# Attention scores of three batches as three half-array products per head, instead of two full-array or one single precision product

## The chip, the core and the metric

The kernel runs on one core of a Trainium2 chip. The metric is the device time of one execution in microseconds, smaller is better. The core's engines run side by side and meet only through semaphores: TensorE (PE: matrix products and transposes, whose weight loads are listed apart as PEld), VectorE (DVE), ScalarE (ACT), GpSimd (POOL), and SyncE (SP), which starts the DMA transfers.

## What is computed

An attention over 4 batches of 8 heads (576 tokens, 64 numbers per head), masked by blocks of 64 tokens, feeds two layers of gated and mixed matrix products:

```python
scores = (q @ k.T) / sqrt(64)            # per batch and head, 576 x 576
scores = where(block_i >= block_j, scores, -1e9)
attn = exp(scores - max(scores)); attn = attn / (sum(attn) + 1e-9)
x = attn @ v                             # 2304 tokens x 512
x = (sigmoid(x @ w_gate) * (x @ w_val)) @ w_out          # first layer, inner width 1536
out = sum over e of p[:, e:e+1] * (relu(x @ w1[e]) @ w2[e])   # second layer, 4 experts of 1024
```

All inputs are single precision. The factors on q and k are such that the scores must be kept to more than one reduced product's precision.

## The kernel before, in words

**Work.** The kernel has three parts. The attention makes x, batch by batch, and writes it to memory (`xd`). The first layer (`l1_1`, `l2_1`) runs in four passes, one for each batch of x; the second layer (`l1_items`, `l2_items`, `l2s_items`) follows. While pass p of the first layer runs, the attention of batch p+1 is woven in: `attn_to` hands out attention steps in proportion to the pass, and a scheduler of the framework then sets the final order on each engine. In pass 0 the weights of the first layer are also read, split into a high and a low part and written back (`raw`, `wa` to `wd`, `wo`).

**Two kinds of product.** TensorE knows a native single precision product (both operands float32), which runs as two passes and has two records in the trace, and a reduced one (float32r). Where precision is wanted from reduced products, a number is split into a high part `hi` and a low part `lo` (the rest), and hi·hi + hi·lo + lo·hi is summed in PSUM. Both layers do that with full-array products (128 rows by 128 columns, 288 to 512 columns streamed).

**Attention, by pairs of heads.** A batch has four pairs (g counts them over all batches: 0 to 15). A pair's q and k come from memory with tokens on partitions (`qn`, `kn`); TensorE transposes them in parts (`prep_tr`, two parts of q, two of k, each into a PSUM bank `tbank`), so that a pair's two heads lie on rows 0-63 and 64-127; ScalarE and VectorE copy them out. Then come the scores by query tile t: t = 0 to 3 have 128 query rows and 128, 256, 384 and 512 key columns, each head for itself, and t = 4 has the last 64 queries of both heads against all 576 keys in two halves of 288 columns. Row maximum (VectorE), exponential (ScalarE), transposes of the result (`pt` into `tbank`), and the product with v (`obank`, two half arrays by columns, native single precision) follow.

Before, the pairs have two forms:

- Form "N" (batches 0 and 1). q and k stay float32, one ScalarE copy for each part. A score tile is one native product on the 64 rows of its head; `side_by_side` puts the two heads' products next to each other, on the upper and lower half of the array. t = 4 is four native products on quarters of the array for each half (64 rows by 64 columns).
- Form "F" (batches 2 and 3). For head h one tile holds q's high part on rows 0-63 and its low part on rows 64-127; the k tile holds the high part twice; a third tile (`klz`) holds k's low part on rows 0-63 and zeros below. So two full-array reduced products give hi·hi + lo·hi and hi·lo. The heads follow one another. The copies out of `tbank` work on 64 rows each: 2 on ScalarE and 2 on VectorE for a part of q, 4 and 2 for a part of k. t = 4 takes four reduced products for each half.

Scores of batches 1 to 3 go to two PSUM banks `s`; the transposes share two banks `t`; the first layer's products use `c1`, `c2` and `lo`. Each `lo` group of six products must wait until VectorE has added the group before it into x (line 884).

**Order.** Every engine works through one queue in the order that the scheduler gave. The attention's steps stand between the first layer's groups of six products.

Of the kernel before, what the change touches and what calls it, by code (L numbers as in the profile page):

```python
# [24 lines left out]
UB = 1  # L25
LATE = (0, 1, 2)
# [36 lines left out]
def attention_moe_moe_kernel(  # L63
# [18 lines left out]
    P = 128  # L82
# [62 lines left out]
    klz = []  # L145
# [6 lines left out]
    def attn_items(segs):  # L152
# [30 lines left out]
        def load(g, nm, src, c0, c1):  # L183
            _, b, pr, seg = pairs[g]
            if nm == "v":
                t = vts[g % 2]
            elif nat_of(g):
                if nm == "k" and pr % 2:
                    t = attn.tile([P, 5 * P], F32, tag="tk", name="kn", bufs=3)
                    t = t.rearrange("p (c h d) -> p c h d", c=5, h=2)  # L190
                else:
                    tag = "kn" if nm == "k" else ("qn", "vn")[pr % 2]
                    t = attn.tile([P, 5, 2, D], F32, tag=tag, name=f"{nm}n")
            else:
                t = attn.tile([P, 5, 2, D], F32, tag=f"{nm}n", name=f"{nm}n")
# [18 lines left out]
        def prep_alloc(g):  # L214
            if nat_of(g):
                prep[g] = dict(
                    tq=attn.tile([P, S], F32, tag="tq", name="tqn", bufs=3),
                    tk=attn.tile([P, 5 * P], F32, tag="tk", name="tkn", bufs=3)[:, :S])
                return
            prep[g] = dict(  # L220
                tq=[attn.tile([P, S], F32R, tag="tq", name="tq", bufs=3) for _ in range(2)],
                tk=[attn.tile([P, 5 * P], F32R, tag="tk", name="tk", bufs=3)[:, :S] for _ in range(2)])

        def prep_tr(g, nm, cs):
# [14 lines left out]
            elif nm == "q":  # L239
                t0, t1 = d["tq"]  # L240
                nc.scalar.activation(out=t0[0:64, sl], in_=tbank[0:64, :o], func=AF.Copy, scale=SCALE)
                nc.scalar.activation(out=t1[0:64, sl], in_=tbank[64:128, :o], func=AF.Copy, scale=SCALE)
                nc.vector.scalar_tensor_tensor(
                    out=t0[64:128, sl], in0=tbank[0:64, :o], scalar=SCALE, in1=t0[0:64, sl].bitcast(F32),
                    op0=ALU.mult, op1=ALU.subtract)
                nc.vector.scalar_tensor_tensor(
                    out=t1[64:128, sl], in0=tbank[64:128, :o], scalar=SCALE, in1=t1[0:64, sl].bitcast(F32),
                    op0=ALU.mult, op1=ALU.subtract)
            else:
# [1184 lines left out]
```

## Time and profile before

| what | value |
|---|---|
| median of 3 runs | 1415.74 us (1414.04 to 1418.02) |
| the profiled execution's own time | 1417.34 us |
| its span in the profile | 1415.6 us |
| TensorE busy / VectorE / ScalarE / GpSimd | 1373.8 / 983.1 / 780.7 / 480.4 us |
| weight loads (PEld) busy | 1266.7 us |
| stretch of the scores of batches 0 and 1 | 8 to 77 us and 77 to 175 us |
| of batches 2 and 3 | 184 to 313 us and 318 to 426 us |

The table is read thus: one engine, TensorE, is busy for 97% of the span; the others have room on average. A busy TensorE is not one at its peak, because a record of a product lasts longer than the distance to the next one. In the rows below the distance between two starts on TensorE is therefore what a piece of work takes, and the middle number of a timeline row (its us) is not.

### The profile page before, as it was taken

How to read it: one execution, taken by the hardware profiler on the slowest of the kernel's cores; microseconds unless marked ns; L12 is line 12 of the kernel's file. 1: busy time of each engine (PE TensorE's matmuls, PEld its weight loads, DVE VectorE, ACT ScalarE, POOL GpSimd, SP SyncE). 2: the span in 40 equal slices, each digit the busy share in tenths (PEclk: the TensorE clock that was granted, in tenths of full speed). 3: DMA queues.
4: the chain of work that ended last, by engine and by line, in shares of the span. 5: the costliest groups of instructions: out<-in, count | busy, mean ns of one | idle time of the engine just before them, and what ended most of it. 6: DMA issues, size and time to landing. Idle time of an engine off the chain costs nothing.

```text
span 1415.6 us, 26232 instructions
## 1 busy us (share of the span) xinstructions
PE 1373.8 (97%) x9212; PEld 1266.7 (89%) x9212; DVE 983.1 (69%) x2103; ACT 780.7 (55%) x1926; POOL 480.4 (34%) x502
## 2 busy tenths in 40 slices
PE   5889999999999999999999999999999999999998
PEld 3447788889899999999999989989999999999998
DVE  6867789986766445467777666757766687766766
ACT  5878788888876433343445445445444454443442
POOL 4544345312112100012576556533322342322322
PEclk8989999999999999999999999999999999999999
DMA  7988787767756888898799888886676777676754
GB/s 227 311 243 277 218 278 264 246 204 214 217 178 229 306 296 267 282 364 311 264 336 358 296 300 302 281 308 227 226 254 249 249 266 278 246 269 231 276 205 157
DMA packets 213683, 371.93 MB, mean 263 GB/s; under 512 B 75568, under 2 KB 140080, under 8 KB 207408
## 3 DMA queue, kind: packets, MB, share of 16 engines
q1 hardware_dynamic: 212464, 369.99, 77.1%
q8 instruction: 74, 1.21, 0.3%
q14 instruction: 57, 0.47, 0.1%
q10 hardware_dynamic: 1088, 0.26, 0.1%
HBM read 269.00 MB, written 101.19 MB: 262 GB/s over the span
## 4 chain that ended last, share of the span: by engine, by line
PE 83%; DMA 5%; DVE 5%; ACT 3%; issue 2%; SPq 1%; POOL 1%; DVEq 0%; ACTq 0%; POOLq 0%
PE c L119 37%; PE o L119 25%; PE lo L119 7%; PE s L119 4%; PE obank L119 3%; PE t L119 2%; PE tbank L458 2%; DMA raw<-in_moe_w_out_dram 1%; DMA raw<-in_moe_w_gate_dram 1%; PE s L349 1%; DMA wa<-w1d 1%; ACT pt L382 1%; DMA w1g<-w1d 1%; PE tbank L229 1%; POOL wt L653 1%
## 5 line engine op out<-in xcount | busy, mean ns | idle before, releaser
L119 PE MATMUL c<-xc,w1g 128*128 128x384 f32 x1920 | 384.8, 338 | 2.1 <-DMA w1g<-w1d 1.8
L119 PEld LDWEIGHTS c<-xc,w1g 128*128 128x128 f32 x1920 | 330.4, 188 | 8.8 <-DVE hb L1062 1.3
L119 PE MATMUL o<-w2s,hb 128*128 128x256 f32 x1728 | 243.5, 282 | 1.1 <-DVE acc L1211 1.1
L119 PEld LDWEIGHTS o<-w2s,hb 128*128 128x128 f32 x1728 | 231.8, 189 | 2.0 <-DVE acc L1211 1.7
L1211 DVE SCALAR_TENSOR_TENSOR acc<-o,pr_t,acc 128x256 f32<-128x256 f32 x264 | 123.4, 479 | 57.9 <-PE o L119 55.7
L1071 POOL TENSOR_TENSOR hs<-hf 128x384 f32<-128x384 f32 x64 | 64.1, 1023 | 287.1 <-ACT hf L1079 255.7
L119 PE MATMUL lo<-g,wo 128*128 128x288 f32 x888 | 148.0, 300 | 4.8 <-DVE x L884 4.8
L119 PE MATMUL o<-w,hb 128*128 128x512 f32 x576 | 142.9, 391 | 0.0
L119 PEld LDWEIGHTS lo<-g,wo 128*128 128x128 f32 x888 | 125.8, 188 | 9.6 <-DVE x L884 6.7
L1079 ACT ACTIVATE hf<-c 128x384 f32<-128x384 f32 x128 | 65.7, 513 | 115.7 <-DVE c L1116 58.4
L119 PEld LDWEIGHTS o<-w,hb 128*128 128x128 f32 x576 | 107.2, 188 | 18.5 <-DVE acc L1155 0.3
L1116 DVE TENSOR_TENSOR c<-c,snap 128x384 f32<-128x384 f32 x144 | 77.9, 553 | 55.8 <-PE c L119 38.9
L1109 ACT ACTIVATE snap<-c 128x384 f32<-128x384 f32 x144 | 65.8, 485 | 85.6 <-PE c L119 85.4
L1060 ACT ACTIVATE hb<-hs 128x384 fp32r<-128x384 f32 x128 | 63.3, 518 | 65.0 <-POOL hs L1071 64.9
L1062 DVE TENSOR_TENSOR hb<-hs,hb 128x384 fp32r<-128x384 f32 x128 | 87.1, 695 | 5.8 <-ACT hb L1060 5.4
L884 DVE TENSOR_TENSOR x<-lo,x 128x288 f32<-128x288 f32 x124 | 55.6, 452 | 45.6 <-PE lo L119 45.0
L119 PE MATMUL c<-xc,wa 128*128 128x288 f32 x504 | 82.6, 299 | 0.9 <-DMA wa<-w1d 0.5
L382 ACT ACTIVATE pt<-s,nm 128x128 f32<-128x128 f32 (+3 forms) x128 | 67.4, 530 | 17.2 <-DVE nm L380 14.5
L119 PEld LDWEIGHTS c<-xc,wa 128*128 128x128 f32 x504 | 71.2, 188 | 3.1 <-DMA wa<-w1d 0.8
L119 PE MATMUL c<-xc,wc 128*128 128x288 f32 x432 | 71.0, 299 | 1.1 <-ACT snap L808 1.1
L458 PE MATMUL tbank<-ident,pt 128*128 128x128 f32 x320 | 55.3, 287 | 17.2 <-ACT pTa L445 9.9
L808 ACT ACTIVATE snap<-c 128x288 f32<-128x288 f32 x108 | 44.2, 409 | 43.8 <-PE c L119 43.2
(173 smaller groups left out, 2697.5 us busy)
## 6 DMA issues: line engine op xcount, KB each, us to landing
w1g<-w1d SPq DMA_DIRECT2D x96, 512.0 KB, 5.4
w2s<-w2d SPq DMA_DIRECT2D x48, 1024.0 KB, 6.5
w1d<-w1g SPq DMA_DIRECT2D x48, 512.0 KB, 5.0
wa<-w1d SPq DMA_DIRECT2D x40, 512.0 KB, 5.2
wb<-w1d SPq DMA_DIRECT2D x40, 512.0 KB, 5.3
wc<-w1d SPq DMA_DIRECT2D x40, 512.0 KB, 4.4
wo<-wod SPq DMA_DIRECT2D x36, 512.0 KB, 6.0
wr<-in_moe_w_dram SPq DMA_DIRECT2D x32, 512.0 KB, 5.4
```

Source lines behind the costliest of these rows:

```text
L119: ins = nc.tensor.matmul(out=out, lhsT=lhsT, rhs=rhs, start=start, stop=stop, skip_group_check=skip)
L382: ins = nc.scalar.activation(out=pt[:, x * nk:(x + 1) * nk], in_=sp[:, x - x0], func=AF.Exp, bias=nm[:, j0 + x:j0 + x + 1], scale=1.0, acc ...
L458: nc.tensor.transpose(out=tbank[:, x * P:(x + 1) * P], in_=pt[:, x * P:(x + 1) * P], identity=ident)
L808: nc.scalar.activation(out=t, in_=d["c1"][:, :TH1], func=AF.Copy)
L884: nc.vector.tensor_tensor(out=x2[t, dm], in0=ps, in1=x2[t, dm], op=ALU.add)
L1060: nc.scalar.activation(out=t[:, 0], in_=src, func=AF.Copy if low is None else AF.Relu)
L1062: nc.vector.tensor_tensor(out=t[:, 1], in0=src, in1=t[:, 0].bitcast(F32), op=ALU.subtract)
L1071: nc.gpsimd.tensor_tensor(out=o, in0=x, in1=y, op=op)
L1079: nc.scalar.activation(out=hf[q, blk], in_=c, func=AF.Relu)
L1109: nc.scalar.activation(out=t, in_=d["c1"][:, :TH], func=AF.Copy)
L1116: nc.vector.tensor_tensor(out=c, in0=d[tag][:, :TH], in1=d[n], op=ALU.add)
L1211: nc.vector.scalar_tensor_tensor(out=o, in0=ps, scalar=pr, in1=o, op0=ALU.mult, op1=ALU.add)
```

## The change

Batch 0 keeps form N. Batches 1, 2 and 3 get a new form "R". q and k of a pair are split into a tile `hi` and a tile `lo` of 128 rows each, with head 0 on the upper and head 1 on the lower 64 rows, by one ScalarE copy and one VectorE subtraction for each part. A score tile is three reduced products for each head on the 64 rows of that head: q-hi with k-hi, q-hi with k-lo, q-lo with k-hi. The heads alternate (head 0, head 1, head 0, ...), each into its own bank, and the first of the six waits until both banks are free. t = 4 becomes three full-array reduced products for each half. `klz` is gone, and q and k of batches 2 and 3 get a second buffer to be loaded into.

```diff
-        QTS = KTS = {"N": range(5), "F": range(5)}
+        QTS = KTS = {"N": range(5), "R": range(5)}
...
         def nat_of(g):
-            return pairs[g][3] != "F"
+            return pairs[g][3] == "N"
...
             prep[g] = dict(
-                tq=[attn.tile([P, S], F32R, tag="tq", name="tq", bufs=3) for _ in range(2)],
-                tk=[attn.tile([P, 5 * P], F32R, tag="tk", name="tk", bufs=3)[:, :S] for _ in range(2)])
+                tq=[attn.tile([P, S], F32R, tag="tq", name="tq", bufs=NB) for _ in range(2)],
+                tk=[attn.tile([P, S], F32R, tag="tk", name="tk", bufs=NB) for _ in range(2)])
...
-            elif nm == "q":
-                t0, t1 = d["tq"]
-                nc.scalar.activation(out=t0[0:64, sl], in_=tbank[0:64, :o], func=AF.Copy, scale=SCALE)
-                nc.scalar.activation(out=t1[0:64, sl], in_=tbank[64:128, :o], func=AF.Copy, scale=SCALE)
+            else:
+                hi, lo = d["tq" if nm == "q" else "tk"]
+                f = SCALE if nm == "q" else 1.0
+                nc.scalar.activation(out=hi[:, sl], in_=tbank[:, :o], func=AF.Copy, scale=f)
                 nc.vector.scalar_tensor_tensor(
-                    out=t0[64:128, sl], in0=tbank[0:64, :o], scalar=SCALE, in1=t0[0:64, sl].bitcast(F32),
-                    op0=ALU.mult, op1=ALU.subtract)
...
+                    out=lo[:, sl], in0=tbank[:, :o], scalar=f, in1=hi[:, sl].bitcast(F32), op0=ALU.mult, op1=ALU.subtract)
...
             with tc.high_priority():
-                two = mms[1][0]()
-            tc.add_manual_dep(two.ins, one.ins.name, NOSYNC, reason="heads side by side")
+                for m in range(1, len(mms) * mms[0][2]):
+                    ins = mms[m % 2][0](m // 2)
+                    tc.add_manual_dep(ins.ins, last.ins.name, NOSYNC, reason="heads side by side")
+                    last = ins
...
-                else:
-                    w = d["tq"][h]
-                    mm("s", out=sp, lhsT=w[:, qs], rhs=d["tk"][h][:, k0:k1], start=True, stop=False)
-                    mm("s", out=sp, lhsT=w[:, qs], rhs=d["kl"][h][:, k0:k1], start=False, stop=True)
+                return nc.tensor.matmul(
+                    out=sp, lhsT=d["tq"][m // 2][r, qs], rhs=d["tk"][m % 2][r, k0:k1], start=(m == 0), stop=(m == 2))
...
-                for n, k in enumerate([*d["tk"], *d["kl"]]):
-                    mm("s", out=sp, lhsT=q4[2 * (g % 2) + n % 2], rhs=k[:, k0:k1], start=(n == 0), stop=(n == 3))
+                for m in range(3):
+                    mm("s", out=sp, lhsT=q4[2 * (g % 2) + m // 2], rhs=d["tk"][m % 2][:, k0:k1], start=(m == 0), stop=(m == 2))
...
-        queue = attn_items([(0, "N"), (1, "N"), (2, "F"), (3, "F")])
+        queue = attn_items([(0, "N"), (1, "R"), (2, "R"), (3, "R")])
```

Because the scheduler sets the order anew, three places are shown as the queues now stand. The first is TensorE's queue at the first tile (t = 0, 128 columns) of batch 2's first pair; `s` are score banks, `c` and `lo` the first layer, `tbank` transposes. Before:

```order
L119 MATMUL s_2775<-tk_2540,tq_2538 128x128
L119 MATMUL s_2775<-klz0_132,tq_2538 128x128
L119 MATMUL s_2781<-tk_2541,tq_2539 128x128
L119 MATMUL s_2781<-klz1_134,tq_2539 128x128
L478 MATMUL tbank_2791<-ident_60,pt4_2550 128x128 x4
```

And in the changed kernel the same tile, where `tq_2634` and `tk_2636` are the high parts, and `tq_2635` and `tk_2637` the low ones:

```order
L120 MATMUL c1_2225<-xc7_1191,wc_2052 128x288 x6
L327 MATMUL s_2865<-tk_2636,tq_2634 128x128
L327 MATMUL s_2866<-tk_2636,tq_2634 128x128
L223 MATMUL tbank_2853<-ident_60,kn_2436 128x128 x3
L327 MATMUL s_2865<-tk_2637,tq_2634 128x128
L327 MATMUL s_2866<-tk_2637,tq_2634 128x128
L327 MATMUL s_2865<-tk_2636,tq_2635 128x128
L327 MATMUL s_2866<-tk_2636,tq_2635 128x128
L445 MATMUL tbank_2900<-ident_60,pt4_2648 128x128 x4
```

The two heads now alternate in two banks, and three full-array transposes stand between the first two products and the last four, so that the tile is two separate half-array blocks. Over the whole queue the 12 pairs of form R have 48 score tiles and 58 such blocks: 10 of the 12 tiles of 128 columns are cut in two in this way. In batch 1 there are 19 of them where 23 native blocks stood before, and in batches 2 and 3 there are 39 where none stood. The blocks of `obank` (half arrays by columns) go from 56 to 60 over the kernel.

The second place is TensorE's queue at the next tile (t = 1, 256 columns) of the same pair. Before:

```order
L119 MATMUL s_2847<-tk_2540,tq_2538 128x256
L119 MATMUL s_2847<-klz0_132,tq_2538 128x256
L119 MATMUL c1_2151<-xc4_1173,wc_1983 128x288 x6
L119 MATMUL s_2853<-tk_2541,tq_2539 128x256
L119 MATMUL s_2853<-klz1_134,tq_2539 128x256
```

And in the changed kernel:

```order
L120 MATMUL lo_2339<-g_1753,wo_1634 128x288 x3
L327 MATMUL s_2939<-tk_2636,tq_2634 128x256
L327 MATMUL s_2940<-tk_2636,tq_2634 128x256
L327 MATMUL s_2939<-tk_2637,tq_2634 128x256
L327 MATMUL s_2940<-tk_2637,tq_2634 128x256
L327 MATMUL s_2939<-tk_2636,tq_2635 128x256
L327 MATMUL s_2940<-tk_2636,tq_2635 128x256
```

The heads, which stood apart with first-layer products between them, are now one block of six.

The third place is VectorE's queue where the first part of k of the same pair is split; `x2` is the sum that releases the bank `lo`. Before:

```order
L884 TENSOR_TENSOR x2_1539<-lo_1971,x2_1539 128x288
L254 TENSOR_TENSOR klz0_132<-tbank_2699,tk_2540 64x256
L255 TENSOR_TENSOR klz1_134<-tbank_2699,tk_2541 64x256
L490 TENSOR_SCALAR nm_2396<-nm_2396 128x4
L491 RECIPROCAL nm_2396<-nm_2396 128x4
L811 TENSOR_TENSOR c_2079<-c2_2058,snap_2050 128x288
L497 COPY xr_2972<-nm_2396 128x256
L884 TENSOR_TENSOR x2_1612<-lo_2004,x2_1612 128x288
```

And in the changed kernel:

```order
L851 TENSOR_TENSOR x2_1775<-lo_2195,x2_1775 128x288
L574 SCALAR_TENSOR_TENSOR raw_2561<-raw_2561 128x512
L457 TENSOR_SCALAR nm_2488<-nm_2488 128x4
L458 RECIPROCAL nm_2488<-nm_2488 128x4
L237 SCALAR_TENSOR_TENSOR tk_2637<-tbank_2797,tk_2636 128x256
L464 COPY xr_3068<-nm_2488 128x256
L851 TENSOR_TENSOR x2_1816<-lo_2255,x2_1816 128x288
```

Between two sums into x one subtraction of 128 rows stands where two of 64 rows stood.

## Rows read from the trace of the kernel before

**Rows 1.** The page's first table: engine, busy us (share of the span), instructions.

```profile
PE 1373.8 (97%) x9212; PEld 1266.7 (89%) x9212; DVE 983.1 (69%) x2103; ACT 780.7 (55%) x1926; POOL 480.4 (34%) x502
```

**Rows 2.** Busy us by stretch: length, PE, PEld, DVE, ACT, POOL, granted clock, DMA.

```profile
97.50:107.80 10.30, 9.62 (x37) 5.29 (x38) 7.20 (x21) 7.51 (x22) 6.32 (x7) 0.50 0.63 192
107.80:180.00 72.20, 69.87 (x490) 54.42 (x488) 53.93 (x136) 59.17 (x167) 26.35 (x28) 1.00 0.80 249
180.00:310.00 130.00, 123.74 (x893) 108.65 (x893) 117.29 (x286) 109.73 (x302) 50.49 (x52) 1.00 0.77 248
310.00:430.00 120.00, 119.95 (x891) 109.21 (x891) 82.66 (x253) 97.89 (x278) 22.90 (x36) 1.00 0.66 201
225.00:265.00 40.00, 35.41 (x256) 30.92 (x255) 37.57 (x84) 32.38 (x87) 23.64 (x24) 1.00 0.78 259
```

**Rows 3.** TensorE's waits, 180 to 310 us: total us, times, longest.

```profile
PE lo L119 <- DVE x L884: 4.4, 5, 1.4
```

**Rows 4.** TensorE's timeline, batch 1, half-array block: start, us, instruction, count.

```profile
158.22 0.96 PE L119 MATMUL c<-xc,wb 128*128 128x288 f32 x6
159.12 0.70 PE L349 MATMUL s<-tkn,tqn 64*128 64x256 f32 x4
159.75 1.06 PE L119 MATMUL c<-xc,wc 128*128 128x288 f32 x6
160.65 0.38 PE L458 MATMUL tbank<-ident,pt 128*128 128x128 f32 x2
```

**Rows 5.** TensorE's timeline, a block of 128 columns in batch 1.

```profile
151.64 0.49 PE L349 MATMUL s<-tkn,tqn 64*128 64x128 f32 x4
152.06 0.66 PE L458 MATMUL tbank<-ident,pt 128*128 128x128 f32 x4
152.48 0.78 PE L119 MATMUL lo<-g,wo 128*128 128x288 f32 x4
```

**Rows 6.** TensorE's timeline, both halves of the last query rows in batch 1.

```profile
166.97 1.19 PE L349 MATMUL s<-tkn,tqn 64*64 64x288 f32 x8
168.08 1.07 PE L119 MATMUL c<-xc,wa 128*128 128x288 f32 x6
```

**Rows 7.** The timeline of the weight loads in the block of rows 4.

```profile
159.11 0.30 PEld L349 LDWEIGHTS s<-tkn,tqn 64*128 64x128 f32 x4 [0.17 <-issue]
```

**Rows 8.** TensorE's timeline in batch 3: score products by width, and their neighbours.

```profile
322.32 0.28 PE L119 MATMUL s<-tk,tq 128*128 128x256 f32 x1
322.44 0.28 PE L119 MATMUL s<-klz,tq 128*128 128x256 f32 x1
...
338.30 0.34 PE L119 MATMUL s<-tk,tq 128*128 128x384 f32 x1
...
338.64 0.95 PE L119 MATMUL c<-xc,wd 128*128 128x288 f32 x6
339.44 0.40 PE L119 MATMUL s<-tk,tq 128*128 128x512 f32 x1
...
339.90 0.97 PE L119 MATMUL lo<-g,wo 128*128 128x288 f32 x6
...
345.67 0.22 PE L119 MATMUL s<-tk,tq 128*128 128x128 f32 x1
...
346.07 0.62 PE L478 MATMUL tbank<-ident,pt 128*128 128x128 f32 x4
346.45 1.04 PE L119 MATMUL lo<-g,wo 128*128 128x288 f32 x6
```

**Rows 9.** VectorE's and TensorE's timelines in batch 2: the wait is in brackets.

```profile
260.02 0.47 DVE L254 TENSOR_TENSOR klz<-tbank,tk 64x320 fp32r<-64x320 f32 x1
260.51 0.49 DVE L255 TENSOR_TENSOR klz<-tbank,tk 64x320 fp32r<-64x320 f32 x1
...
264.47 0.79 PE L119 MATMUL lo<-g,wo 128*128 128x288 f32 x4 [1.23 <-DVE x L884]
```

**Rows 10.** TensorE's timeline before its slow stretch (wait in brackets).

```profile
98.18 1.11 PE L458 MATMUL tbank<-ident,pt 128*128 128x128 f32 x4 [2.32 <-ACT pt L382]
```

More of the change, by code (lines that the diff above doesn't have):

```diff
@@ L25 @@
 UB = 1
+NB = 3
 LATE = (0, 1, 2)
@@ L263, in last_q @@
                 return
+            hi, lo = q4[2 * (g % 2)], q4[2 * (g % 2) + 1]
             for h in range(2):
-                w, r = q4[2 * (g % 2) + h], slice(64 * h, 64 * h + 64)
-                nc.scalar.activation(out=w[0:64, r], in_=src[r], func=AF.Copy, scale=SCALE)
+                r = slice(64 * h, 64 * h + 64)
+                nc.scalar.activation(out=hi[r, r], in_=src[r], func=AF.Copy, scale=SCALE)
                 nc.vector.scalar_tensor_tensor(
-                    out=w[64:128, r], in0=src[r], scalar=SCALE, in1=w[0:64, r].bitcast(F32), op0=ALU.mult, op1=ALU.subtract)
-        first = sum(x[3] != "F" for x in pairs)
+                    out=lo[r, r], in0=src[r], scalar=SCALE, in1=hi[r, r].bitcast(F32), op0=ALU.mult, op1=ALU.subtract)
         seq, start = [], []
@@ L278, in attn_items @@
             seq += [(g, (0, 1), t) for t in qts if t < 2]
-            if pair[3] == "F":
-                seq += [(g, (0,), t) for t in qts if t in (2, 3)]
-                seq += [(g, (0, 1), 4)] * (4 in qts)
-                seq += [(g, (1,), t) for t in qts if t in (2, 3)]
-            else:
-                seq += [(g, (h,), 2) for h in range(2)]
-                seq += [(g, (0, 1), 4)] * (4 in qts)
-                seq += [(g, (h,), 3) for h in range(2)]
+            seq += [(g, (h,), 2) for h in range(2)]
+            seq += [(g, (0, 1), 4)] * (4 in qts)
+            seq += [(g, (h,), 3) for h in range(2)]
         n = len(seq)
@@ L289, in attn_items @@
         st = {}
-        order = {"N": 0, "F": 0}
+        order = {"N": 0, "R": 0}
         ring = []
@@ L306, in s_mm @@
             g, hs, t = seq[i]
-            if nat_of(g) and t in (2, 3):
+            if t in (2, 3):
                 if hs == (0,):
@@ L322, in side_by_side @@
                 return
-            one = mms[0][0]()
-            for _, busy in mms:
+            one = last = mms[0][0](0)
+            for _, busy, _ in mms:
                 if busy:
@@ L359, in scores4 @@
                     return
-                for n, k in enumerate([*d["tk"], *d["kl"]]):
-                    mm("s", out=sp, lhsT=q4[2 * (g % 2) + n % 2], rhs=k[:, k0:k1], start=(n == 0), stop=(n == 3))
+                for m in range(3):
+                    mm("s", out=sp, lhsT=q4[2 * (g % 2) + m // 2], rhs=d["tk"][m % 2][:, k0:k1], start=(m == 0), stop=(m == 2))
             def bank():
-                if native and pairs[g][1] == 0:
+                if pairs[g][1] == 0:
                     nbank[0] += 1
@@ L1251, in l2s_items @@
             return r
-        for x in range(3):
-            t = (attn if x < 2 else pt2).tile([P, S], F32R, tag="kl" if x < 2 else "kl2", name=f"klz{x}", bufs=2 if x < 2 else 1)
-            nc.vector.memset(t[64:128].bitcast(F32), 0.0)
-            klz.append(t)
         for x in range(2):
```

43 lines of the change are left out of this document (8 added, 35 removed).

## The prediction

> **What bounds the kernel now.** I read the page's first table first: TensorE is busy for 97% of the span [rows 1], so what counts is the time that pieces of work take in its queue. An average hides stages, so the second view is the busy time by stretch [rows 2]. There the reader is to compare TensorE with the length of the stretch. From 310 to 430 us (batch 3) it is busy for 119.95 of 120 us: whatever is added to its queue there is added to the end. From 180 to 310 us (batch 2) it is busy for 123.74 of 130, so 6.3 us are idle, and the waits say for whom: VectorE's sum into x, 4.4 us in 5 waits [rows 3]. The short stretch from 225 to 265 us shows why: VectorE is busy for 37.57 of 40 us there and TensorE for 35.41 [rows 2]; for these 40 us VectorE is the bound. The later part of batch 1 (107.8 to 180 us) has 2.3 us of idle in 72.2. After 430 us there is no attention, and the change touches nothing.
>
> The third view is TensorE's timeline around a score tile, read by distances between starts.
>
> **What a half-array block costs.** Six full-array products of 288 columns take 0.80 us, 0.133 each (from 338.64 to 339.44 in [rows 8]). In batch 1 the six before a native block of 256 columns take 0.90, the block 0.63, the six after it 0.90 [rows 4]. A block of 128 columns takes 0.42 [rows 5]. So 128 more columns cost 0.21, which is four columns' time for each at 2.4 GHz (two passes of two); 256 columns are 0.43 of the 0.63, and 0.20 belong to no column. With the two neighbours' 0.10 each a block costs 0.40 us beyond its columns. Where transposes follow, their four take 0.42 [rows 5] and not 0.38 [rows 8], so only 0.04 there; 26 of the 58 new blocks are followed by transposes, and I take 0.38 as the mean. Full-array score products (form F) show nothing of this: the products around them keep 0.80 for six [rows 8].
>
> The Trainium skill, "TensorEngine Tiling (Array Packing)", section Key Properties, says that changing the tiling mode drains TensorE. The trace agrees with a 0.10 us gap ahead of a block and a loss behind it; the page has no price, and by it alone one would only know that the change buys more drains.
>
> **The change, part by part.**
>
> *Full-array pairs of products become blocks (batches 2 and 3, 8 pairs).* Form F's two products for a head take 0.24 us at 256 columns (0.12 each), 0.34 at 384, 0.46 at 512, and the four of both heads 0.40 at 128 [rows 8]. A pair of heads is thus 0.40 + 0.48 + 0.68 + 0.92 = 2.48. In form R the two heads of a step run side by side (native pairs do: otherwise [rows 4, 5] would show eight columns' time, not four), and three steps take 3 x (0.10 + 0.12 + 0.17 + 0.23) = 1.86, if a reduced step in half the array is as long as a full-array one. Gain 0.62 x 8 = 5.0 us. The last query rows: two products of 0.133 fewer in a pair, gain 0.27 x 8 = 2.1 us. Cost: 39 blocks where none stood, 39 x 0.38 = 14.8 us. Together +7.7 us. That it is 39 and not 32 comes from TensorE's new order, where the first tile of a pair is cut in two by transposes.
>
> *Native blocks become reduced blocks (batch 1, 4 pairs).* Streams: native 4 x 1280 columns / 2.4 GHz = 2.13 us for a pair against 1.86 (1280 columns are the four tiles' sum); last query rows 0.91 (1.11 less the 0.20 of a block [rows 6]) against 0.80. Gain 0.38 x 4 = 1.5 us. Blocks: 23 become 19, gain 4 x 0.38 = 1.5 us. Together -3.0 us.
>
> *The scheduler's other moves.* Four more blocks of the product with v, 4 x 0.38 = +1.5 us, at the same price.
>
> TensorE's queue therefore grows by 7.7 - 3.0 + 1.5 = 6.2 us.
>
> *Copies out of the transposes.* In batches 2 and 3 VectorE loses 4 subtractions for a pair (the two longest take 0.47 and 0.49 us [rows 9]; I take 0.45 for each), and ScalarE 8 copies of about as much. Where TensorE is the bound that gives nothing. Where VectorE is the bound it counts twice: [rows 9] show two such subtractions, 0.96 us, in the queue ahead of the sum for which TensorE then waits 1.23 us. The 40 us from 225 to 265 are 40/130 of batch 2, so about 1.2 of its four pairs: VectorE's chain gets 1.2 x 4 x 0.45 = 2.2 us shorter there, and that stretch's share of the new TensorE work (40/130 of 7.7 / 2, so 1.2 us) falls into its idle time. I take 3.4 us as credit. Bounds: no credit, if the new order puts other waits there; at most all 6.3 us of idle time in batch 2. In batch 1 VectorE gains 4 subtractions and 2 small ones a pair, some 8 us in a stretch where it is busy for 53.9 of 72.2 us [rows 2]; I cost them at nothing, because first-layer products fill TensorE's queue while they run; without this cover they cost up to the 2.2 us of one pair.
>
> *New waits.* The first product of a block waits for both `s` banks. Batch 1 already waits so, and has 2.3 us of idle in all [rows 2]; behind the waiting product stand first-layer groups. I cost it at nothing, at most 2.3 us for each batch. The low part of the next pair's q gets a buffer only after the last tile of this pair, and in VectorE's queue it stands just ahead of that tile's row maxima, which wait for the same products: nothing.
>
> *Loads.* The same transfers, into two buffers instead of one; TensorE waits for none of them from 180 us on: nothing.
>
> **The sum.** +6.2 - 3.4 = +2.8 us. The profiled execution took 1417.34 us (span 1415.6), so it would take 1420.1; the median of the runs lies 1.6 us lower, at 1415.74, and becomes 1418.5. A measurement of this kernel can tell about 0.3% (4.2 us) from no change, so the forecast is a loss too small to tell, which stands on a large cost less a large gain.
>
> **The rivals.**
>
> *No credit (slower, about 1421.9).* TensorE's 6.2 us count in full, because VectorE's queue in the new order stalls TensorE elsewhere. For it: where the sums into x stand in the queue is the scheduler's choice. Against it: 225 to 265 us is bound by VectorE, and VectorE loses work. It is slower by over 0.3% from a credit below 2.0 us. Chance 0.20.
>
> *Weights uncovered (slower, about 1426).* If the weights of a head's second and third product could not be loaded while its first streams, each such step would be its columns' time plus a load, an estimate of 0.10 us (half of the block's own 0.20): 0.05 us more at 128 columns, 0.09 at the three others, 0.32 x 2 x 12 pairs = +7.7 us. Against it: all four loads of the 256-column block are done within 0.30 us of its start [rows 7], while its first pass alone, 256 x 2 columns' time or 0.21 us, begins only after a load and so ends later than that. For it: that was a native product. The Trainium skill, "TensorE: Matmul & The Clock Gate", section The mechanism, says that a weight load overlaps with a product in flight only if their row groups differ, which speaks for this rival; the trace does not agree, by the 0.30 us of [rows 7]. Chance 0.08.
>
> *Heads one after the other (slower, about 1441).* If reduced products don't run side by side, the steps double: 12 x 1.86 = +22.3 us. Native ones do [rows 4, 5]. Chance 0.05.
>
> *Blocks cost reduced products nothing (faster, about 1397).* The trace has half-array blocks of native products only. If the 0.38 us belonged to these, 58 x 0.38 = 22 us would go; half of it gives 1408. The loss is gone from 0.05 us less for a block (2.8 / 58), and it is faster by over 0.3% from 0.12. For it: no row shows a reduced product in half an array. Against it: the transposes have single precision operands, and full-array neighbours around them lose next to nothing. Chance 0.08.
>
> *The slow stretch goes, with full credit (faster, about 1411).* From 97.5 to 107.8 us the granted clock is 0.50, the 1.2 GHz level, with TensorE busy for 9.62 of 10.3 us [rows 2]; just before, TensorE had waited 2.32 us for an exponential in batch 1 [rows 10]. Batch 1's order changes, so this can go: 10.3 / 2 = 5.1 us. Alone it gives 1413.4, within 0.3%; with all of batch 2's idle time gone as well, 1415.74 + 6.2 - 6.3 - 5.1 = 1410.5. Chance alone 0.10, with full credit 0.12.
>
> **How the numbers follow.** The forecast has 0.37. Within 0.3%: 0.37 + 0.10 = 0.47. Slower: 0.20 + 0.08 + 0.05 = 0.33. Faster: 0.08 + 0.12 = 0.20. The range leaves out the free blocks below (0.08) and the heads one after the other above (0.05), and reaches from 1410 to 1427; the forecast with its own bounds lies between 1416 and 1422.
>
> **What would show it.** Right: in the timeline of batch 3 a block of six at 256 columns takes about 0.56 us (0.36 + 0.20) from start to next start, and the groups around it 0.90; heads start within 0.01 us of each other; batch 3's stretch is some 4 us longer, with no idle; batch 1's PE work shrinks; from 225 to 265 us less VectorE and less waiting for the sum into x. Wrong: steps of twice the columns' time; groups around a block at 0.80; waits of TensorE for `pt` ahead of a block; the 1.2 GHz stretch gone, longer or moved.

## The result: slower by 0.84%, and the profile after

The changed kernel takes 1429.64 us (median of 6 runs, 1427.73 to 1432.46) against 1417.35 for the kernel before (6 runs, 1414.04 to 1419.06): a ratio of 1.0084, 95% interval 1.0071 to 1.0097. The prediction was 1418.5, in a range up to 1427. The profiled execution took 1430.89 us, with a span of 1429.1, so the span grew by 13.5 us where the sum said +2.8. In runs 8 and 14 below one execution each was slow (3383.09 and 2675.66 us); their medians are of the others.

The page's first table of the changed kernel answers to [rows 1]:

```profile
PE 1381.9 (97%) x9284; PEld 1265.9 (89%) x9284; DVE 976.6 (68%) x2092; ACT 752.9 (53%) x1866; POOL 478.6 (33%) x502
```

TensorE is busy 8.1 us longer than before (1381.9 against 1373.8). The rest of its span is idle: 1429.1 - 1381.9 = 47.2 us, where it was 1415.6 - 1373.8 = 41.8. So the 13.5 us are 8.1 of work and 5.4 of idle time. The prediction had +6.2 of work and 3.4 us less idle time. The work was 1.9 us off, the idle time 8.8 us: in these two executions the fault is mainly in a wait, not in a price. The stretches of the changed kernel answer to [rows 2], with three more behind them (columns as there):

```profile
97.50:107.80 10.30, 7.35 (x38) 4.44 (x38) 8.51 (x26) 9.00 (x30) 5.67 (x7) 0.78 0.72 191
107.80:180.00 72.20, 67.96 (x489) 56.09 (x489) 52.07 (x136) 55.80 (x160) 25.86 (x28) 0.98 0.74 231
180.00:310.00 130.00, 123.84 (x901) 104.96 (x900) 109.21 (x271) 96.48 (x269) 50.03 (x52) 1.00 0.80 259
310.00:430.00 120.00, 120.00 (x893) 103.06 (x892) 72.38 (x225) 79.41 (x234) 16.10 (x29) 1.00 0.63 195
225.00:265.00 40.00, 37.22 (x267) 31.22 (x265) 38.11 (x81) 29.00 (x78) 24.57 (x25) 1.00 0.80 264
60.00:140.00 80.00, 66.69 (x426) 45.43 (x426) 59.94 (x171) 60.50 (x186) 40.04 (x44) 0.91 0.85 263
60.00:520.00 460.00, 436.65 (x3143) 367.89 (x3142) 321.50 (x834) 312.29 (x886) 138.04 (x153) 0.99 0.75 237
430.00:520.00 90.00, 86.31 (x637) 80.47 (x636) 50.66 (x99) 44.62 (x109) 19.07 (x15) 1.00 0.75 245
```

and the same three of the kernel before:

```profile
60.00:140.00 80.00, 72.02 (x463) 46.41 (x461) 58.00 (x162) 64.16 (x194) 35.70 (x39) 0.94 0.88 270
60.00:520.00 460.00, 444.02 (x3177) 382.68 (x3174) 333.23 (x858) 345.57 (x958) 134.33 (x148) 0.99 0.77 246
430.00:520.00 90.00, 89.45 (x667) 87.12 (x667) 46.08 (x86) 41.54 (x96) 12.21 (x8) 1.00 0.83 288
```

From 310 to 430 us TensorE is full as before. From 180 to 310 us it is idle for 6.2 us, as before (6.3), so the credit is not there; from 225 to 265 us VectorE is busy for 38.11 us, no less than in [rows 2]. The new idle time is in two places that the prediction did not name: 60 to 140 us (13.3 us for 8.0) and 430 to 520 us (3.7 for 0.6), where the attention now ends 17 us later: its last product with v starts at 457 us, and stood at 440. From 60 to 520 us TensorE is idle for 23.4 us, and was for 16.0.

The blocks themselves are as forecast. TensorE's timeline of the changed kernel in batch 3 (start, us, instruction, count):

```profile
324.76 0.98 PE L327 MATMUL s<-tk,tq 64*128 64x512 f32 x6
325.67 1.86 PE L120 MATMUL c<-xc,wa 128*128 128x288 f32 x12
...
336.43 0.62 PE L327 MATMUL s<-tk,tq 64*128 64x256 f32 x6
336.98 1.06 PE L120 MATMUL lo<-g,wo 128*128 128x288 f32 x6
337.88 1.76 PE L120 MATMUL c<-xc,wa 128*128 128x288 f32 x12
...
341.24 0.79 PE L327 MATMUL s<-tk,tq 64*128 64x384 f32 x6
341.96 1.33 PE L120 MATMUL c<-xc,wb 128*128 128x288 f32 x8
```

Six products of 256 columns take 0.55 us from start to next start (forecast 0.56), of 384 columns 0.72, of 512 columns 0.91. The group behind a block takes 0.90 us (336.98 to 337.88), the twelve products behind that 1.60, so 0.80 for six.

So what is late in batch 1? TensorE, ScalarE and VectorE of the changed kernel around one change from a pair of heads to the next (wait in brackets; `qn` and `kn` are the next pair's q and k, transposed into `tbank`):

```profile
113.30 0.38 PE L223 MATMUL tbank<-ident,qn 128*128 128x128 f32 x2
113.52 0.60 PE L427 MATMUL tbank<-ident,pt 128*128 128x128 f32 x4
...
116.27 0.38 PE L223 MATMUL tbank<-ident,qn 128*128 128x128 f32 x2
...
119.11 0.96 PE L327 MATMUL s<-tk,tq 64*128 64x512 f32 x6 [0.66 <-ACT pt L384]
...
121.69 0.49 PE L427 MATMUL tbank<-ident,pt 128*128 128x128 f32 x3
123.89 0.41 PE L469 MATMUL tbank<-ident,xr 128*128 128x128 f32 x2 [1.70 <-DVE s L354]
...
127.04 0.38 PE L223 MATMUL tbank<-ident,kn 128*128 128x128 f32 x2
...
128.83 0.33 PE L327 MATMUL s<-tk,tq 64*128 64x128 f32 x2
...
114.59 0.38 ACT L236 ACTIVATE tq<-tbank 128x256 fp32r<-128x256 f32 x1
117.41 0.42 ACT L236 ACTIVATE tq<-tbank 128x256 fp32r<-128x256 f32 x1
...
120.44 0.41 DVE L237 SCALAR_TENSOR_TENSOR tq<-tbank,tq 128x256 fp32r<-128x256 f32 x1
122.76 0.65 DVE L573 TENSOR_SCALAR raw<-raw 128x512 int32<-128x512 int32 x1 [1.90 <-DMA raw<-in_moe_w_gate_dram]
123.33 0.41 DVE L237 SCALAR_TENSOR_TENSOR tq<-tbank,tq 128x256 fp32r<-128x256 f32 x1
```

The two parts of q are transposed at 113.30 and 116.27 us, into both banks `t`, and ScalarE has written the high parts at 114.59 and 117.41. The low parts come only at 120.44 and 123.33, behind this pair's last block (119.11). Until VectorE has read them, both banks are taken: no transpose stands between 116.27 and 121.69 us, and those of the next pair's k go at 127.04, so that its first block starts at 128.83, 9.7 us after the last one. (The second low part also stands behind a conversion of weights that waits 1.90 us for its load, ScalarE waits 3.40 us for the same load, and TensorE's 1.70 us at 123.89 follow from that queue. In run 3 below neither waits for a load there, and the same change still takes 8.9 us.) The low part comes behind the last block at each of the three full changes of pair in batch 1 and at the one into batch 2: blocks at 94.47, 119.11, 150.96 and 182.06 us, low parts at 95.5, 120.4, 152.4 and 183.5. From the last block to the next first one these changes take 5.6, 9.7, 9.3 and 9.6 us, together 34.2; before they took 5.0, 5.3, 6.4 and 10.1, together 26.8. How much of TensorE's idle time comes from that is not read off directly: of the 13.3 us from 60 to 140 us the profile puts only 1.3 down to a part of q on VectorE. That is for the runs to show.

### The profile page after: what moved, and what is told of

It is laid out like the page before. It is cut to its first block, busy times and chain, and to the rows that moved or that the text cites. A ratio compares the mean times of both kernels' runs of the same rounds, so it can differ in the third digit from the quotient of the medians.

```text
span 1429.1 us, 26316 instructions
## 1 busy us (share of the span) xinstructions
PE 1381.9 (97%) x9284; PEld 1265.9 (89%) x9284; DVE 976.6 (68%) x2092; ACT 752.9 (53%) x1866; POOL 478.6 (33%) x502
## 4 chain that ended last, share of the span: by engine, by line
PE 82%; DMA 6%; DVE 5%; ACT 3%; issue 2%; POOL 1%; SPq 1%; DVEq 0%; ACTq 0%; POOLq 0%
PE c L120 36%; PE o L120 26%; PE lo L120 7%; PE s L120 3%; PE obank L120 3%; PE t L120 3%; DMA raw<-in_moe_w_gate_dram 2%; PE tbank L427 2%; PE s L327 1%; DVE raw L574 1%; DMA raw<-in_moe_w_val_dram 1%; DVE raw L573 1%; ACT pt L357 1%; PE tbank L223 1%; DMA wod<-wo 1%
## 5 line engine op out<-in xcount | busy, mean ns | idle before, releaser
L120 PEld LDWEIGHTS o<-w,hb 128*128 128x128 f32 x576 | 107.2, 188 | 18.5 <-DVE acc L1122 0.2
L851 DVE TENSOR_TENSOR x<-lo,x 128x288 f32<-128x288 f32 x124 | 55.5, 452 | 42.0 <-PE lo L120 41.8
L357 ACT ACTIVATE pt<-s,nm 128x128 f32<-128x128 f32 (+3 forms) x128 | 67.1, 529 | 16.9 <-DVE nm L355 13.3
L120 PEld LDWEIGHTS c<-xc,wc 128*128 128x128 f32 x432 | 60.7, 188 | 6.0 <-issue 2.8
```

The source lines that it names most:

```text
L120: ins = nc.tensor.matmul(out=out, lhsT=lhsT, rhs=rhs, start=start, stop=stop, skip_group_check=skip)
L357: ins = nc.scalar.activation(out=pt[:, x * nk:(x + 1) * nk], in_=sp[:, x - x0], func=AF.Exp, bias=nm[:, j0 + x:j0 + x + 1], scale=1.0, acc ...
L851: nc.vector.tensor_tensor(out=x2[t, dm], in0=ps, in1=x2[t, dm], op=ALU.add)
```

## Experiments

Theory: form R keeps two q tiles of a pair, high and low part, in use until the pair's last score tile, out of three buffers; until then the low part of the next pair's q can't be written, the banks `t` stay taken and the next pair's preparation stands still; the attention falls behind in batch 1, and TensorE's queue, which works in order, waits. First rival: the work of the blocks alone. Second rival: VectorE's added subtractions. A third can't be shut out by most of these runs: whatever changes the buffers or the products also makes the scheduler set a new order on every engine, and a new order may gain or lose by itself. For each run "idle" is its span less TensorE's busy time on the page, and "clock" the mean granted clock from 18 to 114 us; the last product with v is placed by the number of first-layer products ahead of it in TensorE's queue.

| run | time us | ratio to before, interval | busy | idle | clock | last v |
|---|---|---|---|---|---|---|
| before | 1417.35 | | 1373.8 | 41.8 | 0.88 | 1380 |
| changed | 1429.64 | 1.0084 (1.0071 to 1.0097) | 1381.9 | 47.2 | 0.88 | 1440 |
| 1 batch 1 native | 1419.99 | 1.0017 (1.0002 to 1.0031) | 1378.7 | 38.1 | 0.89 | 1380 |
| 2 batch 1 alone reduced | 1426.58 | 1.0068 (1.0050 to 1.0086) | 1379.7 | 44.9 | 0.82 | 1464 |
| 3 low part of k first | 1421.50 | 1.0028 (1.0015 to 1.0041) | 1382.4 | 41.6 | 0.84 | 1494 |
| 4 attention ends early | 1424.86 | 1.0054 (1.0036 to 1.0071) | 1380.8 | 41.2 | 0.88 | 1386 |
| 5 four buffers | 1414.01 | 0.9975 (0.9962 to 0.9988) | 1374.9 | 35.4 | 0.89 | 1374 |
| 6 native, subtractions | 1417.07 | 0.9992 (0.9978 to 1.0006) | 1373.7 | 36.4 | 0.95 | 1380 |
| 7 runs 3 and 5 together | 1415.36 | 0.9980 (0.9964 to 0.9996) | 1373.1 | 36.7 | 0.88 | 1374 |
| 8 runs 1, 3 and 5 together | 1421.37 | 1.0026 (1.0010 to 1.0042) | 1376.8 | 38.8 | 0.95 | 1248 |
| 9 q four | 1419.89 | 1.0021 (1.0007 to 1.0034) | 1379.7 | 36.1 | 0.88 | 1368 |
| 10 k four | 1430.77 | 1.0082 (1.0066 to 1.0097) | 1384.8 | 44.1 | 0.88 | 1440 |
| 11 zeros behind | 1428.11 | 1.0070 (1.0056 to 1.0083) | 1388.2 | 39.7 | 0.86 | 1398 |
| 12 zeros between | 1432.53 | 1.0105 (1.0090 to 1.0121) | 1394.9 | 35.2 | 0.89 | 1380 |
| 13 native, two tiles | 1425.31 | 1.0051 (1.0033 to 1.0068) | 1382.8 | 40.1 | 0.89 | 1440 |
| 14 the same, four | 1421.61 | 1.0025 (1.0014 to 1.0036) | 1381.8 | 37.8 | 0.89 | 1300 |

Busy and idle belong to one execution, which in some runs lies some us from the median. The slow clock makes work longer too: 0.01 in the column is at most about 1 us of 96.

### Which batch loses: runs 1 and 2

Run 1 is the changed kernel with

```diff
-        queue = attn_items([(0, "N"), (1, "R"), (2, "R"), (3, "R")])
+        queue = attn_items([(0, "N"), (1, "N"), (2, "R"), (3, "R")])
```

> The changed kernel with batch 1 back in form N (batches 2 and 3 stay in form R). Theory A, the time follows TensorE's queue alone: batch 1 loses the 1.5 us that R's products save there and the queue has 4 more score blocks and 2 fewer blocks of the product with v than the changed kernel, 1.5 + 2 x 0.38 = +2.3, so about 1431.9 us. Theory B, form R in batch 1 delays the attention by its copies and waits, so that it ends late and the end of batch 3 stands idle: batch 1's measured excess (2.9 us) and that after the last product with v (3.7 us) go, about 1423 us. TensorE's queue has the last product with v after 1380 first-layer products, as in the kernel before, where the changed kernel has it after 1440.

It takes 1419.99 us, nearer to B. Run 2 is the kernel before with form R's code for batch 1 alone:

```diff
-        queue = attn_items([(0, "N"), (1, "N"), (2, "F"), (3, "F")])
+        queue = attn_items([(0, "N"), (1, "R"), (2, "F"), (3, "F")])
...
```

> The kernel before with batch 1 alone in form R (batches 2 and 3 stay in form F; k of batch 1 has one load buffer, and four small tiles of the last query rows are cleared on GpSimd between). Theory A, TensorE's queue alone: the predicted gain of batch 1, 3.0 us, about 1414.4 us. Theory B, waits in batch 1 and a late end: the measured 2.9 and 3.7 us stay although batches 2 and 3 are as before, about 1424 us; the last product with v stands after 1464 first-layer products in TensorE's queue.

It takes 1426.58 us. By the ratios form R costs 0.0017 x 1417 = 2.4 us in batches 2 and 3, and alone in batch 1 0.0068 x 1417 = 9.6 us. Not all of the 9.6 need be waiting: the mean clocks of run 2's six executions are 0.984 to 0.987, those of the 22 executions of the kernel before beside them 0.989 to 0.996, and the medians, 0.9865 and 0.993, are up to 0.0065 x 1425 = 9 us of work apart. For the changed kernel (0.986 to 0.991, median 0.989) that is up to 6 us; but its profiled execution and that of the kernel before, 13.5 us apart, have the same 0.991. The stretches of run 1:

```profile
180.00:310.00 130.00, 125.68 (x918) 106.48 (x917) 105.79 (x270) 97.98 (x274) 54.23 (x54) 1.00 0.79 255
225.00:265.00 40.00, 38.79 (x282) 32.08 (x282) 35.26 (x85) 29.56 (x81) 22.60 (x24) 1.00 0.80 264
60.00:140.00 80.00, 71.31 (x445) 44.75 (x445) 60.06 (x159) 61.40 (x190) 40.78 (x44) 0.94 0.85 262
```

From 180 to 310 us it is idle for 4.3 us against 6.3, and VectorE has 35.26 us of work from 225 to 265 for 37.57 [rows 2]: with batch 1 left alone, part of the credit is there. Of the 11 us beyond the forecast 9.5 (0.0084 - 0.0017, times 1417) go with form R in batch 1.

### Smaller causes: runs 3 and 4

```diff
+                x, y = ((0, 1), (1, 0), (0, 0))[m]
                 return nc.tensor.matmul(
-                    out=sp, lhsT=d["tq"][m // 2][r, qs], rhs=d["tk"][m % 2][r, k0:k1], start=(m == 0), stop=(m == 2))
+                    out=sp, lhsT=d["tq"][x][r, qs], rhs=d["tk"][y][r, k0:k1], start=(m == 0), stop=(m == 2))
```

> The changed kernel with the three products of a score tile in another order: the one with the low part of k first, the one with the high parts last. No tile is cut in two any more: 48 blocks in form R for 58, and 57 blocks of the product with v for 60. Theory A, a block costs 0.38 us: 13 fewer give -4.9 us, about 1424.7 us. Theory B, the late end decides: the last product with v moves from 1440 to 1494 first-layer products, so the loss at the end stays or grows and eats most of it, 1428 us or more.

1421.50 us: 8 us less, although the attention ended later still. 13 blocks at 0.38 give 4.9 of it; neither theory has the other 3. And the wait is still there. The same change of pair in this kernel, and TensorE's stretch:

```profile
119.76 0.96 PE L328 MATMUL s<-tk,tq 64*128 64x512 f32 x6
...
121.32 0.74 DVE L237 SCALAR_TENSOR_TENSOR tq<-tbank,tq 128x256 fp32r<-128x256 f32 x2
...
128.69 0.55 PE L328 MATMUL s<-tk,tq 64*128 64x128 f32 x6
...
60.00:140.00 80.00, 69.73 (x449) 48.75 (x450) 63.64 (x177) 63.22 (x193) 41.98 (x45) 0.89 0.85 269
```

The low parts come behind the block, the four changes take 35.2 us, no less than in the changed kernel, and yet TensorE is idle for 10.3 us from 60 to 140 us and not for 13.3. A long change of pair thus costs TensorE time only as its queue stands around it, and not one for one. Run 4:

```diff
-A1 = [1.05, 2.3, 4, 4, 4]
+A1 = [1.05, 2.3, 4.3, 4.3, 4.3]
```

> The changed kernel with the attention of batch 3 handed out faster during the first layer's second pass (target 4.3 for 4 at its end), so that the last product with v stands after 1386 first-layer products for 1440. One score block and 3 blocks of the product with v fewer. Theory A, TensorE's queue alone: -1.5 us, about 1428.1 us. Theory B: the idle time after the end of the attention (3.7 us) goes as well, about 1424.4 us.

1424.86 us, as theory B has it. So an earlier end is worth some 3 to 5 us (the idle time from 430 to 520 us falls only from 3.7 to 2.5 us, so that they are saved there is not shown); but the late end follows from what delays the attention in batch 1, which is the next question.

### Buffers or VectorE's work: runs 5 and 6

```diff
-NB = 3
+NB = 4
```

> The changed kernel with four buffers for the q tiles and four for the k tiles of a pair instead of three, so that the low parts of the next pair need not wait for the last tile of this pair. 51 score blocks of form R for 58, one block of the product with v more; the last product with v stands after 1374 first-layer products for 1440. Theory B1, the third buffer is what delays batch 1: the 7.7 us of idle time that the changed kernel has from 60 to 140 us beyond the run with batch 1 native, most of it, goes, with the late end and 6 blocks: about 1418 to 1420 us. Theory B2, VectorE's subtractions in batch 1 are what delays it: only the blocks (-2.3) and the late end (-3) go, about 1424 us, and the idle time from 60 to 140 us stays above 20 us.

1414.01 us, below every forecast: the whole loss is gone, and the kernel is faster than the one before by 0.25% (0.12 to 0.38). Six blocks fewer are 2.3 of the 15.6 us. The preparation of the same pair in this kernel:

```profile
110.39 0.38 PE L223 MATMUL tbank<-ident,qn 128*128 128x128 f32 x2
...
114.52 0.38 PE L223 MATMUL tbank<-ident,qn 128*128 128x128 f32 x2
...
118.27 0.38 PE L223 MATMUL tbank<-ident,kn 128*128 128x128 f32 x2
...
121.25 0.49 PE L223 MATMUL tbank<-ident,kn 128*128 128x128 f32 x3
121.67 0.96 PE L327 MATMUL s<-tk,tq 64*128 64x512 f32 x6
...
128.14 0.55 PE L327 MATMUL s<-tk,tq 64*128 64x128 f32 x6
...
114.08 0.41 DVE L237 SCALAR_TENSOR_TENSOR tq<-tbank,tq 128x256 fp32r<-128x256 f32 x1
115.77 0.41 DVE L237 SCALAR_TENSOR_TENSOR tq<-tbank,tq 128x256 fp32r<-128x256 f32 x1
```

Both low parts (114.08 and 115.77 us) now lie ahead of the last block (121.67), so do both transposes of k (118.27 and 121.25), and the next pair begins 6.5 us behind the block, not 9.7; its first tile is one block of six where the changed kernel's was cut in two. The four changes of pair take 4.7, 6.5, 5.3 and 7.0 us, together 23.5. The stretches:

```profile
60.00:140.00 80.00, 69.62 (x460) 49.32 (x462) 63.64 (x174) 62.47 (x191) 40.74 (x45) 0.94 0.87 273
60.00:520.00 460.00, 445.25 (x3258) 382.81 (x3259) 324.37 (x849) 316.13 (x895) 137.90 (x152) 0.99 0.77 247
430.00:520.00 90.00, 89.76 (x680) 88.44 (x679) 47.54 (x89) 41.09 (x92) 12.15 (x8) 1.00 0.85 292
```

From 60 to 520 us TensorE is idle for 14.8 us, where it was 23.4 and before the change 16.0; at the end of the attention 0.2 us are left of 3.7. Run 6 puts the work of the subtractions, without the waiting, into run 1:

```diff
+                if pairs[g][1] == 1:
+                    w = attn.tile([P, S], F32, tag="w", name="w", bufs=1)
+                    nc.vector.scalar_tensor_tensor(
+                        out=w[:, sl], in0=tbank[:, :o], scalar=1.0, in1=d["tq" if nm == "q" else "tk"][:, sl], op0=ALU.mult, op1=ALU.subtract)
```

> The run with batch 1 native, and in batch 1 VectorE also makes form R's subtraction of every part of q and k from the transposes' bank, into a tile that nobody reads: VectorE's work and the time that a bank is held are those of form R, but no score waits for it and no buffer is tied up. 75 score blocks for 76 and 61 blocks of the product with v for 58. Theory B2, VectorE's work in batch 1 is the cost: about 1426 us. Theory B1, buffers or the longer chain ahead of the scores: 1420 to 1422 us.

1417.07 us: the rival is dead, and that VectorE's work there costs nothing was right. Why it is even below run 1 is not shown. Its profiled execution had a higher clock (0.95), but over the twelve executions of each the mean clocks are alike, 0.991 to 0.996 here and 0.990 to 0.997 in run 1.

### Together: runs 7 and 8

> The changed kernel with both: the product with the low part of k first (no tile cut in two) and four buffers. 48 score blocks of form R for 58 and 55 blocks of the product with v for 60; the last product with v after 1374 first-layer products. Theory B1: 15 blocks at 0.2 to 0.38 us, the idle time in batch 1 and the end, about 1414 us. Theory B2: about 1420 us.

> Batch 1 in form N, batches 2 and 3 in form R, the product with the low part of k first, four buffers. 56 blocks after batch 0 for the 62 of the run with batch 1 native, 60 blocks of the product with v for 58; the last product with v after 1248 first-layer products for 1380. By blocks alone: 1420.0 - 4 x 0.38 = 1418.5 us. If the earlier end of the attention is worth anything beyond the kernel before, under 1417 us; if the attention's crowding into batch 2 costs waits there, above 1420 us.

Run 7 has nine blocks fewer than run 5 and does not gain (1415.36). It is also run 3 with four buffers, with the same 48 score blocks and 55 blocks of the product with v for 57: 0.0048 x 1417 = 6.8 us less, a second price of the fourth buffer, under half of the first. Run 8 is slower than its blocks say (1421.37): the attention may end too early as well as too late. Both leave some us unexplained, which may be the scheduler's order alone.

### Whose buffers: runs 9 and 10

```diff
-                tq=[attn.tile([P, S], F32R, tag="tq", name="tq", bufs=NB) for _ in range(2)],
+                tq=[attn.tile([P, S], F32R, tag="tq", name="tq", bufs=NB + 1) for _ in range(2)],
...
```

> The changed kernel with a fourth buffer for q's tiles only (three for k's). Theory: the two q tiles of a pair, its high and its low part, are both in use until the pair's last score tile, so that with three of them the low part of the next pair's q waits for that tile; this alone delays the attention. Then the time is that of four buffers for both, 1414 us, within 2. 53 score blocks of form R for 51 and 64 blocks of the product with v for 61 allow 1416. If k's buffers matter as much, about 1422 us.

Run 10 has the same for `tk`.

> The changed kernel with a fourth buffer for k's tiles only. All five engines' queues are those of the changed kernel, row for row. Theory (q's buffers are the cause): the changed kernel's time, 1429.6 us within 1.5. If k's buffers matter: well below, to 1420 us.

q's fourth buffer takes 0.63% off (1.0084 to 1.0021, 8.9 us), k's nothing (1430.77, with every queue in the changed kernel's order). q's alone falls 6 us short of run 5, where 2 were allowed: its queue has 5 more blocks (2 us), the rest is not accounted for.

The four changes of pair, read in every run as above, fall into two groups. With form R in batch 1 and three buffers for q they take 34.2 to 37.6 us (the changed kernel, runs 2, 3, 4 and 10). With four buffers, or with batch 1 native as in runs 1 and 6, they take 22.8 to 25.5 us (runs 1, 5 to 9, 11, 12 and 14). So that three buffers make the changes long is shown; what a long change costs in time differs from order to order, as run 3 says.

### What a block costs: runs 11 and 12

Run 5 with one product more for each score block of batches 2 and 3, by a tile of zeros, so that the sum stays the same. In run 11 `m == 5`, in run 12 `m == 3`:

```diff
+                    if mms[0][3] and m == 3:
+                        ins = mms[0][3](m == 5)
+                        tc.add_manual_dep(ins.ins, last.ins.name, NOSYNC, reason="heads side by side")
+                        last = ins
...
```

> The kernel with four buffers for both, and in batches 2 and 3 a full-array product with a tile of zeros, of the tile's width, behind each of the 32 score blocks (it adds nothing to the sum). It stands next to other full-array work and cuts no block: 8 x 1280 columns / 2.4 GHz = 4.3 us and about 0.01 us each, so 1414.0 + 4.6 = about 1418.6 us; it is the base for the next run.

> The same, but the product with zeros stands in the middle of each block, between the fourth and the fifth product, so each of the 32 blocks of batches 2 and 3 is two; 34 more blocks in all than in the run with the zeros behind. If a half-array block of reduced products costs the predicted 0.38 us: 34 x 0.38 = +12.9 us over that run, about 1431.5 us; without its last part, where products of the same mode follow, 0.30 us, so at least +10 us. If blocks cost reduced products nothing: the same time as that run.

Run 11 took 1428.11, 14 us over run 5 and not 4.6: its order is another, with idle time of 39.7 us for 35.4 and a lower clock, and 2 us or so have no name. As the base for run 12 it is spoilt, and the difference of 4.4 us would be 0.13 for a block. Run 12's idle time and clock are those of run 5, so I compare these two: +18.5 us, of which 4.6 are the zeros themselves, and 13.9 / 34 = 0.41 us for each block (an estimate; the two intervals leave 0.32 to 0.49). The timelines decide it. Run 11, 384 columns, zeros behind:

```profile
341.48 0.79 PE L332 MATMUL s<-tk,tq 64*128 64x384 f32 x6
342.20 0.44 PE L336 MATMUL s<-tk,zero 128*128 128x384 f32 x1
342.48 0.56 PE L120 MATMUL c<-xc,wc 128*128 128x288 f32 x3
342.88 0.96 PE L120 MATMUL lo<-g,wo 128*128 128x288 f32 x6
```

and run 12, zeros between:

```profile
331.19 0.62 PE L332 MATMUL s<-tk,tq 64*128 64x384 f32 x4
331.74 0.44 PE L336 MATMUL s<-tk,zero 128*128 128x384 f32 x1
332.11 0.44 PE L332 MATMUL s<-tk,tq 64*128 64x384 f32 x2
332.47 0.66 PE L120 MATMUL lo<-g,wo 128*128 128x288 f32 x3
332.98 0.38 PE L477 MATMUL tbank<-ident,xr 128*128 128x128 f32 x2
```

Run 11 needs 1.00 us from the block's start to the next first-layer group and 0.40 for three of its products; run 12 needs 1.28 and 0.51. The same work costs 0.39 us more when it is cut once. Over all blocks of the two runs that first-layer products follow, the medians say 0.40 us at 256 columns, 0.39 at 384, 0.38 at 512 and 0.28 at 128.

### Held buffers without form R: runs 13 and 14

Four buffers change the order of every queue. Here batch 1 stays native but holds buffers as form R does: two full copies of q and of k for a pair, one for each head.

```diff
+                    x = "2" if pairs[g][1] == 1 and h else ""
-                    return nc.tensor.matmul(out=sp, lhsT=d["tq"][r, qs], rhs=d["tk"][r, k0:k1], start=True, stop=True)
+                    return nc.tensor.matmul(out=sp, lhsT=d["tq" + x][r, qs], rhs=d["tk" + x][r, k0:k1], start=True, stop=True)
...
```

> Batch 1 in form N, but with two full copies of q and of k (one by ScalarE, one by VectorE), head 0 multiplying the one and head 1 the other: the products are the native ones, and the buffers are taken and held as in form R, two q tiles and two k tiles until the pair's last score tile, out of three each. 79 score blocks and 61 blocks of the product with v, for 75 and 61 in the run with unused subtractions; the last product with v after 1440 first-layer products, as in the changed kernel. Theory, the held buffers are the cost whatever the products are: 1417.1 + 1.5 for blocks + most of the 9 us = about 1426 us. Rival, the three products with their chain (high part, low part, product) are the cost: 1417 to 1420 us.

(The queue has 57 blocks of the product with v, not 61.)

> The same with four buffers for q's and for k's tiles. Theory: the loss of the run before goes, 1417 to 1419 us. Rival: no difference to the run before beyond 2 us.

Run 13 takes 1425.31 us, and in its queue the attention ends after 1440 first-layer products, as in the changed kernel, without a single reduced product in batch 1. Run 14 takes 1421.61, above its forecast. Four buffers thus take 3.7 us away. The loss that they are to be held against is 8.4 us by run 6 (0.59%; run 14 keeps 0.33%), from which the forecasts started, and 4.8 by run 1 (0.34%; run 14 keeps 0.08%). So held buffers cost time whatever the products are, but the fourth buffer gives back only part of it for certain. Nor do the 3.7 us stand where the theory has them: from 60 to 140 us TensorE is idle for 9.3 us in run 13 and 10.5 in run 14. The four changes of pair take 29.7 and 24.6 us.

## Why the prediction was wrong, point by point

**The step that failed** stands under new waits: "The low part of the next pair's q gets a buffer only after the last tile of this pair, and in VectorE's queue it stands just ahead of that tile's row maxima, which wait for the same products: nothing." The wait was seen and priced by what stands on VectorE beside it. What I did not follow is what that q holds meanwhile: both transpose banks, and so every transpose behind. The four changes of pair get 34.2 - 26.8 = 7.4 us longer, TensorE is idle for 5.3 us more from 60 to 140 us, and the attention ends 17 us later. Cost, where the sum has nothing: 8.9 us by run 9, all of the loss and more by run 5; with other products 6.8 (runs 3 and 7) and 3.7 (runs 13 and 14). The sign is the same in all four pairs of runs, but all four also change the order of the queues, so the size of the step in the changed kernel is not exact, and the way from the long changes to TensorE's idle time is in part argued. Form F had the same number of q tiles and did not suffer so: in its code each tile belongs to one head, the heads follow one another, and the first is free after that head's last 512-column tile. That the heads alternate is what ties up both to the end; I argue this from the code, no run tried it.

**Batch 1's -3.0 us** came out as +9.6 (run 2): by its changes of pair (34.7 us) the same step, with more time at the 1.2 GHz level, which the sum had nothing for. The 8 us of VectorE's work at nothing was right (run 6).

**The block price** of 0.38 to 0.40 us was right: 0.39 by the rows of runs 11 and 12 (0.28 at 128 columns), 0.41 by the times of runs 5 and 12. So were the streams, the heads side by side, and the covered weights. The Trainium skill, "TensorEngine Tiling (Array Packing)", section Key Properties, names the drain; the runs here give its price. The Trainium skill, "TensorE: Matmul & The Clock Gate", section The mechanism, would let a weight load overlap only where row groups differ; here the three steps of a head, all on the same rows, follow one another at their columns' time (a block of 256 columns takes 0.55 us, 3 x 0.12 and one overhead), so the trace does not agree with that sentence; the same section also lets a load go ahead into a background weight buffer, which the trace does not contradict. TensorE's work grew by 8.1 us where 6.2 were forecast.

**The credit of 3.4 us** did not show in the changed kernel, as the rival without credit had it; in run 1 the idle time from 180 to 310 us is 2.0 us smaller, and over the whole span 3.7 us (38.1 for 41.8). Batches 2 and 3 alone were forecast at 7.7 - 3.4 = +4.3 us; run 1 gives +2.4 (0.3 to 4.4).

**The rivals.** Weights uncovered came nearest in time (1426), and is wrong: the blocks have no 0.05 to 0.09 us more for a step. Free blocks and heads in turn are refuted by the block rows. The slow clock from 97.5 to 107.8 us did shrink (0.78), but other stretches took its place; the mean from 18 to 114 us is 0.88 in both.

**Still open** is why run 3 gains 3 us more than its blocks, why run 9 falls 6 us short of run 5 and why run 11 loses 14 where its zeros cost 4.6: each changes the scheduler's order everywhere, and what blocks and zeros don't explain reaches some 9 us. No run gave q a fourth buffer and kept the changed kernel's order, which would tell the wait from the order.

## What to carry to other kernels

When operands of a step become several tiles that are all in use to the step's end, count buffers for two steps, not tiles for one and a half: a shared ring that was enough while the tiles came free one by one becomes a wait once they come free together. Price a wait by what the waiting operand holds (here both banks of the transposes) and by what is queued behind that, not by its neighbour in the same queue. And where a scheduler orders everything anew, undo the suspected wait (one more buffer) before believing a price: here one constant turned +0.84% into -0.25%. The order moves with it, so repeat the test on a variant: the same constant was worth 15.6 us here and 6.8 with the products in another order.

## What the runs showed of the hardware

A half-array block between full-array products costs the same beyond its columns whether its products are native (0.40 us, [rows 4]) or reduced in three steps (0.39, runs 11 and 12), and reduced products in the two halves run side by side at one column rate (in the block at 336.43 us of the changed kernel the heads start 3 ns apart).

How long TensorE runs at the 1.2 GHz level differs between executions of one kernel: the mean clocks of run 1's twelve go from 0.990 (1423.29 us) to 0.997 (1418.11 us). Between 18 and 114 us the profiled executions of runs 1 and 6 have 0.89 and 0.95, so up to 0.06 x 96 = 5.8 us of one execution hang on where these stretches fall. Why they fall there no run shows.
